# Splitting the first projection into q and k, spreading bit moves, and issuing two pairs of block loads later, in an attention kernel with a feed-forward part

## The chip, the cores and the metric

The kernel runs on one core of a Trainium2 chip. The metric is the device time of one execution in microseconds (us); lower is better. A core has five engines that run side by side: TensorE (PE, matrix products; its weight loads are listed apart as PEld), VectorE (DVE), ScalarE (ACT), GpSimd (POOL) and SyncE (SP, which here only issues transfers). The span of a profile is about 1.8 us shorter than the time of the same run, so spans are compared with spans and times with times.

## The reference

```python
# q, k, v: 4 batches x 8 heads x 768 x 64; proj: 64 x 6
q_bits = (einsum('bhsd,dk->bhsk', q, proj) > 0)      # 6 sign bits of each row
k_bits = (einsum('bhsd,dk->bhsk', k, proj) > 0)
mask   = bucket(q_bits)[..., :, None] == bucket(k_bits)[..., None, :]
scores = where(mask, q @ k.T / sqrt(64), -1e9)
x      = softmax(scores) @ v                          # 3072 tokens x 512
h      = x @ w_in                                     # 512 -> 2048
out    = (h * sigmoid(h)) @ w_out                     # 2048 -> 512
```

The mask is put into the score product as extra rows: the six bits of each row of q and k stand beside its 64 values (a contraction of 71 rows for the very first head, of 128 for most). So before a head's scores can be computed, its q and k must be transposed, projected by `proj`, compared with a threshold (which makes the bits), and the bits moved to their rows. Two heads make a pair; there are 16 pairs.

## The kernel before

The first head has code of its own, since nothing can run before its scores. One PSUM tile takes four projection products, for the two halves (e) of q and k (n), each 32 rows tall:

```python
def proj_first(h):
    bp = ps.tile([P, 512], F32, tag="m", name="bp_ps", bufs=3)
    for c in range(4):
        e, n = divmod(c, 2)
        x0 = (2 * h + n) * HS
        o = e * (NBIT + 1)
        nc.tensor.matmul(bp[32 * c : 32 * c + 32, 0:HS], pw[:, o : o + 32],
                         qk32[0][:, x0 : x0 + HS], start=True, stop=True)
    bt = btp.tile([P, S], F16, tag="bits", name="bits")
    nc.vector.tensor_scalar(out=bt[:, 0:HS], in0=bp[:, 0:HS], ...)   # one threshold
    return bt
# ... (cut)
t_first(0, 0, nc.scalar.copy)            # q of head 0: transposes on PE, copy on ACT
t_first(0, 1, nc.vector.tensor_copy)     # k of head 0: copy on DVE
warm_up(2)                               # products that compute nothing
bt = proj_first(0)
v_unit(0, (0,))                          # POOL: cast and sums of v
# ... casts on ACT, four bit moves on DVE, DVE, ACT and POOL (cut)

def second_head():
    bt = proj_first(1)
    # ... casts on POOL, four bit moves on DVE, v_unit (cut)
```

Later pairs are prepared in units planned between the attention units of earlier heads. For a group Q of four heads' worth of columns (two pairs), in `w0 = (Q - 1) * QST`:

```python
for i in range(4 if Q > 2 else 0):
    w1 = w0 + (5, 9, 11, 14)[i]
    plan(w1, lambda Q=Q, i=i: block_unit(2 * Q + i // 2, i % 2))   # DVE transpose of a block
plan(w0 + 20, lambda Q=Q: proj_unit(2 * Q, 2 * Q + 1))
for i in range(4):
    plan(w0 + 20, lambda Q=Q, i=i: bits_unit((2 * Q, 2 * Q + 1), i // 2, i % 2))
# ... (cut)
    plan(w0 + (20 if Q == 3 else 8) + i, lambda p=2 * Q + 2 + i: load_blocks(p))
```

A `bits_unit` is two DVE operations of 13 x 768 elements. In between, DVE also multiplies out the gates `g` of the feed-forward part, and each g frees a PSUM tile that PE needs for the next product `h_ps`. `x_unit(p)` writes the attention output of pair p, which SP then transposes into `xT` by a transfer.

Of the kernel before, what the change touches and what calls it, by code (L numbers as in the profile page):

```python
# [9 lines left out]
F32 = mybir.dt.float32  # L10
# [3 lines left out]
ALU = mybir.AluOpType  # L14
# [3 lines left out]
def kernel(  # L18
# [10 lines left out]
    nc = tc.nc  # L29
    B, H, S, D = q.shape  # L30
    NBIT = proj.shape[1]
    NT, DMODEL = out.shape
    DFF = moe_w_in.shape[1]
    P = 128
# [12 lines left out]
    cst = ctx.enter_context(tc.tile_pool(name="cst", bufs=1))  # L47
# [5 lines left out]
    nrm = ctx.enter_context(tc.tile_pool(name="nrm", bufs=2))  # L53
# [10 lines left out]
    v_sb = {}  # L64
# [21 lines left out]
    def load_blocks(p):  # L86
        b, h0 = p // 4, 2 * (p % 4)
        for n, src in (("q", q), ("k", k)):
            t = ld.tile([P, NG, 32], F32, tag=f"ld{n}", name=f"{n}_blk")
            for j in range(4):  # L90
                i, half = divmod(j, 2)
                nc.sync.dma_start(  # L92
                    out=t[32 * j : 32 * j + 32],
                    in_=src[b, h0 + i].rearrange("(r g) d -> r g d", r=32)
                    [:, :, 32 * half : 32 * half + 32])
            qk_sb[p, n] = t
# [18 lines left out]
    pw = cst.tile([P, 40], F32, name="pw")  # L115
# [7 lines left out]
    def warm_up(n):  # L123
        for _ in range(n):
            nc.tensor.matmul(wps, warm, warm[:, None, :].to_broadcast([P, 4, P]),  # L125
                             start=True, stop=True)
# [7 lines left out]

    NR = 2 * NBIT + 1
    BIG = 1e30
    sc = cst.tile([P, 3], F32, name="sc")
    for j, val in enumerate((0.0, 0.5, 1.0)):
        nc.vector.memset(sc[:, j : j + 1], val)
    for c in range(4):  # L140
        one = (-BIG, 0.0) if c % 2 == 0 else (BIG, 0.25 * NBIT)
        for n, val in ((NBIT + 1, one), (NBIT, (0.0, 0.5))):
            for j in range(2):
                nc.vector.memset(sc[32 * c : 32 * c + n, j : j + 1], val[j])
        if c % 2:
            nc.vector.memset(sc[32 * c : 32 * c + NBIT, 2:3], 0.0)

# [4 lines left out]
    NVS = 8  # L152
    VV = [cst.tile([P, NJ, E1], F16, name=f"vv{i}") for i in range(NVS)]
    VS = [cst.tile([P, 2, E1], F16, name=f"vs{i}") for i in range(NVS // 2)]
# [36 lines left out]
    HS = S // 2  # L191

    def t_first(h, n, copy):
        if (h, n) == (0, 0):
            qk32[0] = t32.tile([P, 2 * S], F32, tag="qk32", name="qk32")
        tp = ps.tile([P, 512], F32, tag="m", name="tp_ps", bufs=3)
        for j in range(NJ // 2):
            nc.tensor.transpose(tp[:, j * P : (j + 1) * P],  # L198
                                qk_sb[0, "qk"[n]][:, h, j * P : (j + 1) * P], ident)
        x0 = (2 * h + n) * HS  # L200
        copy(out=qk32[0][:, x0 : x0 + HS], in_=tp[:, 0:HS])

    def halves(t, r, n, e):

        return t[r, n * S : (n + 1) * S].rearrange("d (x e c) -> d x e c", e=2, c=P)[:, :, e]

    def cast_first(h, n, e, eng):
        dst = halves(QKA[0], slice(0, D), n, e) if h == 0 else \
            halves(QKB[0], slice(D, 2 * D), n, e)
        x0 = (2 * h + n) * HS  # L210
        src = qk32[0][e * D : (e + 1) * D, x0 : x0 + HS].rearrange("d (x c) -> d x c", c=P)
        if eng is nc.scalar:
            eng.mul(dst, src, CS)
        else:
            eng.tensor_scalar(out=dst, in0=src, scalar1=CS, scalar2=1.0,
                              op0=ALU.mult, op1=ALU.mult)

    def proj_first(h):

        bp = ps.tile([P, 512], F32, tag="m", name="bp_ps", bufs=3)  # L220
        for c in range(4):
            e, n = divmod(c, 2)
            x0 = (2 * h + n) * HS
            o = e * (NBIT + 1)
            nc.tensor.matmul(bp[32 * c : 32 * c + 32, 0:HS], pw[:, o : o + 32],  # L225
                             qk32[0][:, x0 : x0 + HS], start=True, stop=True)
        bt = btp.tile([P, S], F16, tag="bits", name="bits")
        nc.vector.tensor_scalar(out=bt[:, 0:HS], in0=bp[:, 0:HS],
                                scalar1=sc[:, 0:1], scalar2=sc[:, 1:2],
                                op0=ALU.is_gt, op1=ALU.subtract)  # L230
        return bt

    def bits_first(bt, h, n, e, copy):
        c = 2 * e + n
        r = slice(32 * c, 32 * c + NBIT + 1)
        dst = halves(QKA[0], slice(D, D + NBIT + 1), n, e) if h == 0 else \
            halves(QKB[0], slice(0, NBIT + 1), n, e)
        copy(out=dst, in_=bt[r, 0:HS].rearrange("d (x c) -> d x c", c=P))  # L238

    def block_unit(p, n):  # L240
        if n == 0:
            qk32[p] = t32.tile([P, 2 * S], F32, tag="qk32", name="qk32")

        dst = qk32[p][:, n * S : (n + 1) * S].rearrange(
            "p (t r a) -> p a t r", t=NJ, r=32, a=4)
        nc.vector.transpose(out=dst, in_=qk_sb[p, "qk"[n]])  # L246

    def cast_unit(p, par):
        sl = p % NSL
        dst, rows = ((QKA[sl], slice(0, 64)), (QKB[sl], slice(64, 128)))[par]  # L250
        nc.gpsimd.tensor_scalar(out=dst[rows, :], in0=qk32[p][rows, :],  # L251
                                scalar1=CS, scalar2=1.0,
                                op0=ALU.mult, op1=ALU.mult)

    def v_unit(p, heads=(0, 1)):
        for i in heads:
            h = 2 * p + i
            vv, vs = VV[h % NVS], VS[p % (NVS // 2)]
            src = v_sb[p][:, i, :].rearrange("p (t d) -> p t d", d=D)
            nc.gpsimd.tensor_copy(out=vv[:, :, 0:D], in_=src)  # L260
            sa = nrm.tile([P, 3, D], F32, tag="vsa", name="vsa")
            nc.gpsimd.tensor_tensor(out=sa, in0=src[:, 0:3], in1=src[:, 3:6], op=ALU.add)  # L262
            sb = nrm.tile([P, D], F32, tag="vsb", name="vsb")
            nc.gpsimd.tensor_tensor(out=sb, in0=sa[:, 0], in1=sa[:, 1], op=ALU.add)
            nc.gpsimd.tensor_tensor(out=vs[:, i, 0:D], in0=sb, in1=sa[:, 2], op=ALU.add)

    bits = {}

# [229 lines left out]

    t_first(0, 0, nc.scalar.copy)
    t_first(0, 1, nc.vector.tensor_copy)  # L500
    warm_up(2)
    bt = proj_first(0)
    v_unit(0, (0,))
    for e in range(2):
        for n in range(2):
            cast_first(0, n, e, nc.scalar)
    for e in range(2):
        for n in range(2):
            bits_first(bt, 0, n, e, (nc.vector.tensor_copy, nc.vector.tensor_copy,
                                     nc.scalar.copy, nc.gpsimd.tensor_copy)[2 * e + n])  # L510
    t_first(1, 0, nc.vector.tensor_copy)
    t_first(1, 1, nc.vector.tensor_copy)
    warm_up(3)

    def second_head():
        bt = proj_first(1)
        for e in range(2):
            for n in range(2):
                cast_first(1, n, e, nc.gpsimd)
                bits_first(bt, 1, n, e, nc.vector.tensor_copy)  # L520
        v_unit(0, (1,))

    at = {}
# [1 line left out]
    def plan(w, fn):  # L525
        at.setdefault(w, []).append(fn)


    plan(1, second_head)
    for i in range(3):  # L530
        plan(4 + 2 * i, lambda i=i: t_unit(1, i))
    for i in range(2):
        plan(8, lambda i=i: cast_unit(1, i))
        plan(8, lambda i=i: v_unit(1, (i,)))
# [28 lines left out]
    for Q in range(2, NQUAD):  # L563
        w0 = (Q - 1) * QST
        for i in range(4 if Q > 2 else 0):
            w1 = w0 + (5, 9, 11, 14)[i]
            plan(w1, lambda Q=Q, i=i: block_unit(2 * Q + i // 2, i % 2))
            if i % 2:
                for par in range(2):
                    plan(w1, lambda p=2 * Q + i // 2, par=par: cast_unit(p, par))  # L570
        plan(w0 + 20, lambda Q=Q: proj_unit(2 * Q, 2 * Q + 1))
        for i in range(4):
            plan(w0 + 20,
                 lambda Q=Q, i=i: bits_unit((2 * Q, 2 * Q + 1), i // 2, i % 2))
        for i in range(2):
            plan(w0 + 5 + i, lambda p=2 * Q + i: load_v(p))
            for j in range(2):
                plan(w0 + 18 + 9 * i + 2 * j, lambda p=2 * Q + i, j=j: v_unit(p, (j,)))
            if Q + 1 < NQUAD:
                plan(w0 + (20 if Q == 3 else 8) + i, lambda p=2 * Q + 2 + i: load_blocks(p))  # L580
    for p in range(NPAIR):
        plan((30, 42, 58)[p] if p < 3 else 2 * NU * (p + 1) + (2 if p % 4 == 3 else 9),
             lambda p=p: x_unit(p))
# [5 lines left out]
    for w in range(NW):  # L589
# [9 lines left out]
        n = -(-(len(moeq) - keep) // left) if len(moeq) > keep else 0  # L599
# [3 lines left out]
        if n == 1 and len(moeq) - keep < left and skip:  # L603
            n = 0
# [43 lines left out]
```

## Time and profile before

| | before |
|---|---|
| time, 3 runs | 307.0 us median (306.68 to 307.44) |
| the profiled run and its span | 308.2 us, span 306.4 us |
| PE busy | 299.8 us, 98% of the span |
| DVE, ACT, POOL busy | 59%, 69%, 42% |
| PE idle before h_ps | 1.03 us at 66.85 and 1.38 us at 76.14 |
| first scores, first exponentials, first u products | 7.94, 8.35, 9.00 us |

PE is nearly always busy, so DVE, ACT or POOL time matters only where PE stands still for it.

### The profile page before, as it was taken

The page shows a single profiled execution, that of the slowest core. Times are in us where ns is not written, and L with a number is a line of the kernel's source. Part 1 is how long each engine was busy: PE and PEld are TensorE (multiplying, and loading weights), DVE is VectorE, ACT ScalarE, POOL GpSimd, SP SyncE. Part 2 cuts the span into 40 slices and gives each one's busy share as a digit, 9 for nine tenths or more (in the row PEclk, how much of TensorE's full clock was granted, in tenths as well). Part 3 has the DMA queues.
Part 4 walks back from the last instruction along what each step waited for, and adds up shares of the span by engine and source line. Part 5 has one row for each costly group of instructions (what it writes and reads, how often), then busy time and mean ns, then how long its engine had stood idle before and what let it go on. Part 6 is the DMA issues. An engine that isn't in the chain of part 4 may idle for free.

```text
span 306.4 us, 7166 instructions
## 1 busy us (share of the span) xinstructions
PE 299.8 (98%) x2710; PEld 174.8 (57%) x2710; DVE 181.8 (59%) x342; ACT 210.2 (69%) x391; POOL 128.9 (42%) x203
## 2 busy tenths in 40 slices
PE   8999999988999999999999999999999999999996
PEld 3675855544666555545565665545566664446653
DVE  5797977789559534854597325864453342664332
ACT  5887989987777686878876666778877731543200
POOL 7589999368514842765138431675111100000000
PEclk9999999999999999999999999999999999999999
DMA  7999797999939825774048434111022013001112
GB/s 201 243 263 208 139 134 115 184 247 169 167 91 174 153 65 158 125 135 127 9 92 131 89 64 148 52 41 33 2 60 62 0 37 94 34 2 68 36 60 76
DMA packets 102786, 32.87 MB, mean 107 GB/s; under 512 B 90656, under 2 KB 99808, under 8 KB 102752
## 3 DMA queue, kind: packets, MB, share of 16 engines
q1 hardware_dynamic: 98368, 28.22, 42.8%
q0 software_dynamic: 4224, 4.19, 9.2%
q8 instruction: 21, 0.34, 0.5%
q14 instruction: 13, 0.11, 0.1%
q10 hardware_dynamic: 160, 0.00, 0.0%
HBM read 27.27 MB, written 6.29 MB: 110 GB/s over the span
## 4 chain that ended last, share of the span: by engine, by line
PE 89%; DVE 4%; DMA 4%; ACT 1%; SPq 1%; issue 0%; POOL 0%; ACTq 0%; POOLq 0%
PE o_ps L455 26%; PE h_ps L423 24%; PE s_ps L333 18%; PE o_ps L365 12%; DMA k_blk<-in_k_dram 4%; PE bp_ps L279 3%; PE tp_ps L185 2%; DVE g L429 1%; PE o_ps L441 1%; PE warm_ps L125 1%; PE tp_ps L198 1%; DVE qka L310 1%; PE bp_ps L225 1%; ACT u L336 1%; SPq L92 1%; DVE qk L246 1%
## 5 line engine op out<-in xcount | busy, mean ns | idle before, releaser
L336 ACT ACTIVATE u<-s_ps 128x512 f16<-128x512 f32 x288 | 156.3, 605 | 40.3 <-PE s_ps L333 39.8
L429 DVE SCALAR_TENSOR_TENSOR g<-th,h_ps 128x512 f16<-128x512 f32 x96 | 65.1, 684 | 75.9 <-ACT th L427 75.9
L423 PE MATMUL h_ps<-xT,win 128*128 128x512 f16 (+1 forms) x512 | 97.4, 325 | 2.4 <-DVE g L429 2.4
L365 PEld LDWEIGHTS <-u 128*128 128x128 f16 x1152 | 67.5, 98 | 42.8 <-ACT u L336 11.2
L455 PE MATMUL o_ps<-wout,g 128*128 128x512 f16 x368 | 91.6, 379 | 0.0
L427 ACT ACTIVATE th<-h_ps 128x512 f32<-128x512 f32 x96 | 57.3, 597 | 39.2 <-PE h_ps L423 36.0
L365 PE MATMUL o_ps<-vv,u 128*128 128x65 f16 x1152 | 82.8, 194 | 0.2
L423 PEld LDWEIGHTS <-win 128*128 128x128 f16 x512 | 49.9, 98 | 34.3 <-issue 3.0
L385 POOL TENSOR_TENSOR x_pr<-osum,rec 128x384 f16<-128x384 f32 x23 | 19.0, 824 | 90.5 <-DVE rec L384 90.1
L455 PEld LDWEIGHTS <-g 128*128 128x128 f16 x368 | 35.8, 98 | 34.1
L333 PE MATMUL s_ps<-qkb 128*128 128x512 f16 x192 | 52.8, 326 | 0.0
L333 PE MATMUL s_ps<-qka 71*128 71x512 f16 x192 | 52.7, 327 | 0.1
L251 POOL TENSOR_SCALAR qka<-qk 64x1536 f16<-64x1536 f32 x15 | 21.9, 1462 | 13.4 <-DVE qk L246 8.3
L460 DVE TENSOR_SCALAR osb<-o_ps 128x512 f32<-128x512 f32 x23 | 15.8, 685 | 15.5 <-PE o_ps L455 15.5
L251 POOL TENSOR_SCALAR qkb<-qk 64x1536 f16<-64x1536 f32 x15 | 22.0, 1468 | 1.2
L262 POOL TENSOR_TENSOR vsa<-v_sb 128x192 f32<-128x192 f32 x32 | 19.5, 609 | 0.0
L260 POOL CAST vv<-v_sb 128x384 f16<-128x384 f32 x32 | 16.4, 514 | 0.9 <-DMA v_sb<-in_v_dram 0.5
L246 DVE STREAM_TRANSPOSE qk<-k_blk 128x768 f32<-128x768 f32 x10 | 15.7, 1575 | 1.4 <-DMA k_blk<-in_k_dram 1.4
L333 PEld LDWEIGHTS <-qka 71*128 71x128 f16 x192 | 15.4, 97 | 0.7 <-ACT qka L238 0.5
L246 DVE STREAM_TRANSPOSE qk<-q_blk 128x768 f32<-128x768 f32 x10 | 15.7, 1574 | 0.0
L333 PEld LDWEIGHTS <-qkb 128*128 128x128 f16 x192 | 15.4, 97 | 0.0
L379 DVE TENSOR_TENSOR osum<-o_ps,vsum 128x390 f32<-128x390 f32 x23 | 13.0, 565 | 2.3
(64 smaller groups left out, 165.3 us busy)
## 6 DMA issues: line engine op xcount, KB each, us to landing
out_dram<-osb SPq DMA_DIRECT2D x23, 256.0 KB
v_sb<-in_v_dram SPq DMA_DIRECT2D x15, 384.0 KB
q_blk<-in_q_dram SPq DMA_DIRECT2D x40, 96.0 KB
k_blk<-in_k_dram SPq DMA_DIRECT2D x40, 96.0 KB
win<-in_moe_w_in_dram POOLq DMA_DIRECT2D x4, 512.0 KB, 6.9
wout<-in_moe_w_out_dram POOLq DMA_DIRECT2D x4, 512.0 KB, 7.4
q_sb<-in_q_dram SPq DMA_DIRECT2D x5, 384.0 KB
k_sb<-in_k_dram SPq DMA_DIRECT2D x5, 384.0 KB
```

Source lines behind the costliest of these rows:

```text
L246: nc.vector.transpose(out=dst, in_=qk_sb[p, "qk"[n]])
L251: nc.gpsimd.tensor_scalar(out=dst[rows, :], in0=qk32[p][rows, :], scalar1=CS, scalar2=1.0, op0=ALU.mult, op1=ALU.mult)
L260: nc.gpsimd.tensor_copy(out=vv[:, :, 0:D], in_=src)
L262: nc.gpsimd.tensor_tensor(out=sa, in0=src[:, 0:3], in1=src[:, 3:6], op=ALU.add)
L333: nc.tensor.matmul(sp[:, o0 : o0 + n], t[rows, S + jt * P : S + (jt + 1) * P], t[rows, c0 : c0 + n], start=True, stop=True)
L336: nc.scalar.activation(out=u, in_=sp, func=AF.Exp, scale=ESC)
L365: nc.tensor.matmul(o_ps[h][:, c0 // P + i, :], u[:, o0 + i * P : o0 + (i + 1) * P], vv[:, jt, :], start=(not direct(h) and w % NU == 0 and ...
L385: (nc.vector if direct(h) else nc.gpsimd).tensor_tensor(out=x_pr[p][:, :, par * D : (par + 1) * D], in0=o[:, 0:NJ, 0:D], in1=rec[:, :, Non ...
L423: nc.tensor.matmul(hp[:, j, :], w_in16[:, dt, ft * P : (ft + 1) * P], xT[4 * b + dt][:, c0 : c0 + n], start=(dt == 0), stop=(dt == NDT - 1))
L427: nc.scalar.activation(out=th, in_=hp, func=AF.Tanh, scale=0.5)
L429: after.append(lambda: nc.vector.scalar_tensor_tensor(out=g[ci][:, grp * f : (grp + 1) * f, :], in0=th, scalar=1.0, in1=hp, op0=ALU.add, o ...
L455: nc.tensor.matmul(o2[tt], g[ci][:, ft, ct * P : (ct + 1) * P], w_out16[:, ft, :], start=(ft == 0), stop=(ft == NFT - 1))
```

## The change

The intent: let q of the first head go through projection, threshold and bit moves while k is still being copied; spread the eight bit moves of a group over four units instead of one, so that gates can run between them; transpose blocks one unit later; and issue the block loads of pairs 8 and 9 behind the transfer of x of pair 4. The core of the diff:

```diff
-    sc = cst.tile([P, 3], F32, name="sc")          # constants of the thresholds
+    sc = cst.tile([P, 7], F32, name="sc")
... (20 more memsets)
-    def proj_first(h):
+    def proj_first(h, n):
         bp = ps.tile([P, 512], F32, tag="m", name="bp_ps", bufs=3)
-        for c in range(4):
-            e, n = divmod(c, 2)
+        for e in range(2):
+            o = e * (NBIT + 1)
             x0 = (2 * h + n) * HS
-            o = e * (NBIT + 1)
-            nc.tensor.matmul(bp[32 * c : 32 * c + 32, 0:HS], pw[:, o : o + 32],
+            nc.tensor.matmul(bp[32 * e : 32 * e + 32, 0:HS], pw[:, o : o + 32],
                              qk32[0][:, x0 : x0 + HS], start=True, stop=True)
... (threshold of 64 partitions in place of 128)
-    warm_up(2)
-    bt = proj_first(0)
-    v_unit(0, (0,))
+    bq = proj_first(0, 0)
+    warm_up(1)
+    bk = proj_first(0, 1)
... (casts of q on ACT, of k on POOL; moves of q on POOL and ACT, of k on DVE and ACT)
+    v_sums(0, 0)                                    # behind the bits on POOL
...
     def second_head():
-        bt = proj_first(1)
+        bt = [proj_first(1, n) for n in range(2)]
...
-            w1 = w0 + (5, 9, 11, 14)[i]
+            w1 = w0 + (5, 9, 12, 15)[i]
...
-            plan(w0 + 20,
+            plan(w0 + 20 + (i if Q < 4 else 0),
                  lambda Q=Q, i=i: bits_unit((2 * Q, 2 * Q + 1), i // 2, i % 2))
...
-                plan(w0 + (20 if Q == 3 else 8) + i, lambda p=2 * Q + 2 + i: load_blocks(p))
+                plan(w0 + (28 if Q == 3 else 8) + i, lambda p=2 * Q + 2 + i: load_blocks(p))
```

More of the change, by code (lines that the diff above doesn't have):

```diff
@@ L136 @@
     BIG = 1e30
-    sc = cst.tile([P, 3], F32, name="sc")
-    for j, val in enumerate((0.0, 0.5, 1.0)):
+    sc = cst.tile([P, 7], F32, name="sc")
+    for j, val in enumerate((0.0, 0.5, 1.0, 0.0, 0.5, 0.0, 0.5)):
         nc.vector.memset(sc[:, j : j + 1], val)
@@ L144 @@
                 nc.vector.memset(sc[32 * c : 32 * c + n, j : j + 1], val[j])
+        if c < 2:
+            for m, n, val in ((3, NBIT + 1, (-BIG, 0.0, BIG, 0.25 * NBIT)),
+                              (3, NBIT, (0.0, 0.5, 0.0, 0.5))):
+                for j in range(4):
+                    nc.vector.memset(sc[32 * c : 32 * c + n, m + j : m + j + 1], val[j])
         if c % 2:
@@ L216, in cast_first @@
                               op0=ALU.mult, op1=ALU.mult)
-    def proj_first(h):
+    def proj_first(h, n):
         bp = ps.tile([P, 512], F32, tag="m", name="bp_ps", bufs=3)
-        for c in range(4):
-            e, n = divmod(c, 2)
+        for e in range(2):
+            o = e * (NBIT + 1)
             x0 = (2 * h + n) * HS
-            o = e * (NBIT + 1)
-            nc.tensor.matmul(bp[32 * c : 32 * c + 32, 0:HS], pw[:, o : o + 32],
+            nc.tensor.matmul(bp[32 * e : 32 * e + 32, 0:HS], pw[:, o : o + 32],
                              qk32[0][:, x0 : x0 + HS], start=True, stop=True)
         bt = btp.tile([P, S], F16, tag="bits", name="bits")
-        nc.vector.tensor_scalar(out=bt[:, 0:HS], in0=bp[:, 0:HS],
-                                scalar1=sc[:, 0:1], scalar2=sc[:, 1:2],
+        nc.vector.tensor_scalar(out=bt[0:64, 0:HS], in0=bp[0:64, 0:HS],
+                                scalar1=sc[0:64, 3 + 2 * n : 4 + 2 * n],
+                                scalar2=sc[0:64, 4 + 2 * n : 5 + 2 * n],
                                 op0=ALU.is_gt, op1=ALU.subtract)
@@ L233, in bits_first @@
     def bits_first(bt, h, n, e, copy):
-        c = 2 * e + n
-        r = slice(32 * c, 32 * c + NBIT + 1)
+        r = slice(32 * e, 32 * e + NBIT + 1)
         dst = halves(QKA[0], slice(D, D + NBIT + 1), n, e) if h == 0 else \
@@ L253, in cast_unit, with v_sums @@
                                 op0=ALU.mult, op1=ALU.mult)
+    def v_sums(p, i):
+        vs = VS[p % (NVS // 2)]
+        src = v_sb[p][:, i, :].rearrange("p (t d) -> p t d", d=D)
+        sa = nrm.tile([P, 3, D], F32, tag="vsa", name="vsa")
+        nc.gpsimd.tensor_tensor(out=sa, in0=src[:, 0:3], in1=src[:, 3:6], op=ALU.add)
+        sb = nrm.tile([P, D], F32, tag="vsb", name="vsb")
+        nc.gpsimd.tensor_tensor(out=sb, in0=sa[:, 0], in1=sa[:, 1], op=ALU.add)
+        nc.gpsimd.tensor_tensor(out=vs[:, i, 0:D], in0=sb, in1=sa[:, 2], op=ALU.add)
     def v_unit(p, heads=(0, 1)):
         for i in heads:
-            h = 2 * p + i
-            vv, vs = VV[h % NVS], VS[p % (NVS // 2)]
             src = v_sb[p][:, i, :].rearrange("p (t d) -> p t d", d=D)
-            nc.gpsimd.tensor_copy(out=vv[:, :, 0:D], in_=src)
-            sa = nrm.tile([P, 3, D], F32, tag="vsa", name="vsa")
-            nc.gpsimd.tensor_tensor(out=sa, in0=src[:, 0:3], in1=src[:, 3:6], op=ALU.add)
-            sb = nrm.tile([P, D], F32, tag="vsb", name="vsb")
-            nc.gpsimd.tensor_tensor(out=sb, in0=sa[:, 0], in1=sa[:, 1], op=ALU.add)
-            nc.gpsimd.tensor_tensor(out=vs[:, i, 0:D], in0=sb, in1=sa[:, 2], op=ALU.add)
+            nc.gpsimd.tensor_copy(out=VV[(2 * p + i) % NVS][:, :, 0:D], in_=src)
+            v_sums(p, i)
     bits = {}
@@ L500 @@
     t_first(0, 1, nc.vector.tensor_copy)
-    warm_up(2)
-    bt = proj_first(0)
-    v_unit(0, (0,))
+    bq = proj_first(0, 0)
+    warm_up(1)
+    bk = proj_first(0, 1)
     for e in range(2):
-        for n in range(2):
-            cast_first(0, n, e, nc.scalar)
+        cast_first(0, 0, e, nc.scalar)
+    nc.gpsimd.tensor_copy(out=VV[0][:, :, 0:D],
+                          in_=v_sb[0][:, 0, :].rearrange("p (t d) -> p t d", d=D))
     for e in range(2):
-        for n in range(2):
-            bits_first(bt, 0, n, e, (nc.vector.tensor_copy, nc.vector.tensor_copy,
-                                     nc.scalar.copy, nc.gpsimd.tensor_copy)[2 * e + n])
+        cast_first(0, 1, e, nc.gpsimd)
+    bits_first(bq, 0, 0, 0, nc.gpsimd.tensor_copy)
+    bits_first(bq, 0, 0, 1, nc.scalar.copy)
+    bits_first(bk, 0, 1, 0, nc.vector.tensor_copy)
+    bits_first(bk, 0, 1, 1, nc.scalar.copy)
+    v_sums(0, 0)
     t_first(1, 0, nc.vector.tensor_copy)
@@ L519, in second_head @@
                 cast_first(1, n, e, nc.gpsimd)
-                bits_first(bt, 1, n, e, nc.vector.tensor_copy)
+                bits_first(bt[n], 1, n, e, nc.vector.tensor_copy)
         v_unit(0, (1,))
```

## The prediction

> **What bounds the kernel now.** I read the page's busy shares first, then the chain of waits in order of time, then the timelines of the stretches where TensorE (PE) is named as having sat idle. PE is busy 299.8 of 306.4 us, and from 76 us on the chain is PE work almost without a break, so time is won only where PE stands still. There are two such places: the start, and 64 to 77 us. First the start, in the timelines of VectorE (DVE), ScalarE (ACT) and GpSimd (POOL), and of PE:
>
> ```profile
> 4.86 0.56 DVE L201 COPY qk<-tp_ps 128x384 f32<-128x384 f32 x1 [0.84 <-PE tp_ps L198]
> 6.38 0.68 DVE L228 TENSOR_SCALAR bits<-bp_ps,sc 128x384 f16<-128x384 f32 x1 [0.96 <-PE bp_ps L225]
> 7.09 0.70 DVE L238 COPY qka<-bits 7x384 f16<-7x384 f16 x2
> ...
> 5.45 1.48 ACT L213 ACTIVATE qka<-qk 64x384 f16<-64x384 f32 x3 [0.20 <-DVE qk L201]
> ...
> 6.12 0.32 POOL L265 TENSOR_TENSOR vs<-vsb,vsa 128x64 f16<-128x64 f32 x1
> ...
> 7.94 0.81 PE L333 MATMUL s_ps<-qka 71*128 71x512 f16 x4
> ```
>
> The columns are start, duration, engine, line, operation, tiles, count, and the idle time before with its releaser. One projection tile holds q and k, so its threshold waits until 6.38 for all four products; the bit moves end at 7.79 and the first scores start at 7.94. Next the middle, in the chain of waits and in the timelines of DVE and PE:
>
> ```profile
> 52.54 12.14 DMA k_blk<-in_k_dram
> 64.69 0.02 issue
> 64.71 1.57 DVE qk L246
> ...
> 74.06 0.64 DVE qkb L310
> 74.70 0.01 issue
> 74.71 0.65 DVE qkb L307
> 75.36 0.03 issue
> 75.40 0.70 DVE g L429
> 76.10 0.04 issue
> 76.14 1.02 PE h_ps L423 x4
> ```
>
> ```profile
> 66.85 1.02 PE L423 MATMUL h_ps<-xT,win 128*128 128x512 f16 x4 [1.03 <-DVE g L429]
> 76.14 1.02 PE L423 MATMUL h_ps<-xT,win 128*128 128x512 f16 x4 [1.38 <-DVE g L429]
> ```
>
> The last quarter of k of pair 7 lands at 64.69. DVE then works without a break for 11.4 us: a transpose, gates (g), a head's sums, thresholds, and all eight bit moves of pairs 6 and 7 in one block. PE needs a PSUM tile that only a g frees, and waits 1.03 and then 1.38 us. Later the page names no PE wait of any size.
>
> **What the Trainium skill says.** "DMA: Bandwidth & Descriptors", section "Queues, rings and completion order", has each DMA engine consume one ring in order and go round robin, packet by packet, between queue rows. The trace agrees: I counted its packet records. The 128-byte packets of the block loads (SP's queue) run at about 900 per us until 54 us, then at about 180 per us beside 175 per us of 1 KB weight packets (GpSimd's queue), until 64. So the late landing comes from the weight loads of w_in 2 and 3 and w_out 0, which POOL issues at 51.8 to 54.2; the blocks of pairs 8 and 9 stand behind pair 7 in the same ring. "GPSIMD Engine Reference", section "1. Specifications", has GpSimd share its SBUF interfaces with VectorE. In this trace the last bit multiplication took 0.65 us beside POOL sums, but 0.41 us for pair 6 just before; I use the slower figure.
>
> **The change part by part.** The instruction order of the built kernel, compared with this one's, shows what really moves.
>
> 1. Constants: 20 more DVE memsets (4 full columns, 16 short ones). The 16 short ones before take 0.87 us, 0.054 each, so 20 cost at most 1.1; unwaited ones start 0.015 to 0.03 apart, so 0.6 to 0.9 is likelier. DVE has 0.84 us idle before its copy at 4.86. Cost 0, at worst 0.2.
>
> 2. First head. The q projection runs right behind the transposes of k: PE is free at 4.82 (chain), and q was copied at 4.70. Four products took 0.78 in the second head (chain), so two take 0.4: done about 5.3. DVE thresholds q after its copy of k (ends 5.42): 5.45 to 6.13, as 64 partitions of 384 should take the 0.68 that 128 do. PE does one warm-up matmul, then the k products from 5.5 to 5.93. Threshold of k: 6.05 to 6.73, since back-to-back pairs start about 0.6 apart. Moves: q on ACT at 6.15 (0.51), done 6.66; k on ACT 6.75 to 7.26 and on DVE 6.75 to 7.14. POOL: v cast to 5.09, two k casts from 5.46 (before, four took 2.16, so 0.54 each) to 6.54, one q move (0.50) to 7.05. The last move ends at 7.26 instead of 7.79; scores start near 7.35, 0.55 us earlier.
>
> 3. The price. The sums of v go behind the bits on POOL. From the start of vsa to the end of vs took 1.39 us (5.05 to 6.44), so they end at 7.05 + 1.4 = 8.45. The first instruction of the attention product (the small constant matmul that reads vs, 0.17 us on the chain) cannot start before, and the u matmuls follow at about 8.7. They started at 9.00; without this wait it would have been 8.4. So 0.3 of the 0.55 us survives. From 9.00 to 50 us PE and ACT carry the chain, so I pass on 0.3.
>
> 4. Second head: two thresholds instead of one, about 0.6 us more of DVE, partly hidden because q's products are ready 0.4 earlier. The bits are wanted at 12.95 and were done at 12.52; 0.2 us later is still in time. Cost 0.
>
> 5. Block transposes one unit later: the order on DVE, PE and POOL does not change at all by this. Effect 0.
>
> 6. Bit moves one per unit. Around pairs 4 and 5 one xT copy moves ahead of two bit moves; PE is not waiting there. Around pairs 6 and 7 exactly one g moves ahead of the last two bit operations. It ran at 75.40, and its tanh was done at 71.94, so it now runs at 74.08 to 74.76, when PE is just free (76.14 - 1.38 = 74.76). That wait goes. But the second g is still behind the two bit operations: 74.70 + 0.65 + 0.65, so 76.05 to 76.73, while PE would want it at 74.80 + 1.20 = 76.0. A new wait of about 0.7 us appears. That next product starts at 76.75 instead of 77.34: gain 0.6, at most 0.8.
>
> 7. Blocks of pairs 8 and 9 behind x of pair 4. SP issued them from 57.10 to 82.19 and x at 82.29. Now SP stands still until x of head 9 is written (POOL, 70.26 to 71.08), and the blocks go out from about 72. For pairs 10 and 11 sixteen such DMAs needed 13.5 us (90.41 to 103.76); with two weight loads still in flight I take 16, so the last lands near 88 to 90. DVE wants the four tiles at 90.70, 94.59, 96.02 and 98.64, in the order in which they land (about 80, 83, 86, 90). Slack over 7 us. As they never delayed pair 7, moving them frees nothing on the path: 0.
>
> Sum: 0.3 at the start, 0.6 to 0.8 at 76 us, no loss: about 1.0 us. 307.0 - 1.0 = 306.0.
>
> **The rivals.** A: the block move is the real gain. If pairs 8 and 9 do take bandwidth from pair 7, k of pair 7 lands up to 4 us earlier, the 1.03 us wait and the rest of the second go, and the time is about 304.3. For it: the change's own title, and the overlap of their issue (57.10 on) with the landing. Against it: no packet of pairs 8 and 9 moved before 64.7, and one ring is served in order. B: the landing is a race between POOL's weight loads and SP's blocks. Some 1,500 packets of pair 7 were left when the weights began. Weights half a microsecond later would let some 400 packets by at full rate, and k would land about 2 us earlier; weights sooner would cost little, as they end at 64 anyway. Both issue times follow from the same start, so I expect them to shift alike, but this race makes the lower side of the range longer. C: the start's 0.3 us is lost by 65 us, because DVE works on from a landing that did not shift: 306.4. D: the delayed blocks stall DVE at 90 us, a microsecond or two lost: 307 to 308. The slack of 7 us speaks against it. E: the constants or the v sums eat the start's gain: 306.4.
>
> **Range and chances.** Most cases lie between C and the full sum with 0.3 us more, 305.5 to 306.5. The three runs before spread by 0.76 us, and A and B reach down to 304.3, so I set 305.0 to 306.9. Two per cent is 6.1 us, over twice all PE waits named (1.03 + 1.38 and half a microsecond of start), so faster by that much is nearly out of the question, and slower needs a stall nothing shows.
>
> **What would show it.** The first scores start at about 7.35 and the first u matmuls at about 8.7, after a wait on vs of GpSimd; if they start at 8.4, step 3 is wrong. The wait of 1.38 us before h_ps is replaced by one of about 0.7 us a product later; the 1.03 us wait stays. K of pair 7 lands at 64.4 within 0.5; a landing at 62 or before would mean A or B. DVE never waits on q or k blocks of pairs 8 and 9. From 80 us on each product starts about 1 us earlier than before, and that offset stays to the end.

## More of the kernel before

The page's list of the chain that ended last, by engine, for this kernel:

```profile
PE 89%; DVE 4%; DMA 4%; ACT 1%; SPq 1%; issue 0%; POOL 0%; ACTq 0%; POOLq 0%
```

The 4% DMA are the one landing (k of pair 7) that the prediction quotes.

## The result, and the profile after

The changed kernel takes 307.45 us (median of 4 runs, 307.07 to 307.61); the kernel before, in the same rounds, 306.84 us (4 runs, 306.62 to 307.44). The ratio is 1.0015, with a 95% interval of 0.9997 to 1.0033. A ratio here is the mean time of one kernel's runs over that of the other's of the same rounds, so it is not quite the ratio of the medians. The class "within 2%" is right. The predicted 306.0 us is not, and 307.45 lies outside the range of 305.0 to 306.9: a gain of 1.0 us was expected and none came.

The changed kernel's start, in the timelines of PE, DVE, POOL and ACT (start, duration, engine, line, operation, tiles, count, and the idle time before with its releaser):

```profile
4.99 1.19 PE L230 MATMUL bp_ps<-qk,pw 128*32 128x384 f32 x4
6.44 0.84 PE L230 MATMUL bp_ps<-qk,pw 128*32 128x384 f32 x4
8.57 0.81 PE L341 MATMUL s_ps<-qka 71*128 71x512 f16 x4
9.64 0.30 PE L373 MATMUL o_ps<-vv,u 128*128 128x65 f16 x4
10.08 1.48 PE L230 MATMUL bp_ps<-qk,pw 128*32 128x384 f32 x8
...
6.22 0.67 DVE L233 TENSOR_SCALAR bits<-bp_ps,sc 64x384 f16<-64x384 f32 x1 [0.71 <-PE bp_ps L230]
7.32 0.67 DVE L233 TENSOR_SCALAR bits<-bp_ps,sc 64x384 f16<-64x384 f32 x1 [0.43 <-PE bp_ps L230]
...
8.66 0.32 POOL L267 TENSOR_TENSOR vs<-vsb,vsa 128x64 f16<-128x64 f32 x1
```

The first scores start at 8.57 us instead of 7.94, and not at 7.35 as predicted. The two products of q (four records: each float32 product shows as two passes) take 1.19 us, those of k 0.84; the prediction had 0.4 for either. The second head's products take 1.48 us at 10.08; all four took 0.85 us before. The threshold of k at 7.32 follows its products, and it is later than the one threshold of before at 6.38.

The middle of the changed kernel, in the timelines of DVE and PE:

```profile
73.83 0.69 DVE L437 SCALAR_TENSOR_TENSOR g<-th,h_ps 128x512 f16<-128x512 f32 x1
74.54 0.39 DVE L318 COPY qkb<-bits 13x768 f16<-13x768 f16 x1
74.94 0.42 DVE L315 TENSOR_SCALAR qkb<-bits,sc 13x768 f16<-13x768 f16 x1
75.39 1.28 DVE L437 SCALAR_TENSOR_TENSOR g<-th,h_ps 128x512 f16<-128x512 f32 x2
...
74.67 1.03 PE L431 MATMUL h_ps<-xT,win 128*128 128x512 f16 x4
76.13 1.02 PE L431 MATMUL h_ps<-xT,win 128*128 128x512 f16 x4
```

One g has moved ahead of the last two bit operations, just as predicted, and neither product shows a wait: one of 0.15 us or more would stand in brackets at the end. (The second product does have a shorter one; see bits_only.) The chain that ended last has lost its DMA part:

```profile
PE 94%; DVE 2%; ACT 1%; issue 1%; POOL 0%; ACTq 0%; POOLq 0%
```

The block loads, in the timeline of SP's issues and of DVE:

```profile
70.86 1.46 SPq L408 DMA_TRANSPOSE xT<-x_pr  x1
72.41 4.27 SPq L92 DMA_DIRECT2D q_blk<-in_q_dram  x4
...
89.49 1.56 DVE L251 STREAM_TRANSPOSE qk<-q_blk 128x768 f32<-128x768 f32 x1
```

The loads of pairs 8 and 9 do start only at 72.41, behind x of pair 4, and end their issue at 88.86; DVE takes the first block at 89.49 without a wait for it.

Against the first profile of the kernel before, the exponentials of the changed kernel run 1.27 us late from the fifth one on (12.05 against 10.78), and yet its span is 1.1 us shorter. That puzzle was the first thing to settle.

### The profile page after: what moved, and what is told of

The parts are those of the page before. It is cut to its first block, busy times and chain, and to the rows that moved or that the text cites. A ratio compares the mean times of both kernels' runs of the same rounds, so it can differ in the third digit from the quotient of the medians.

```text
span 305.3 us, 7187 instructions
## 1 busy us (share of the span) xinstructions
PE 300.9 (99%) x2709; PEld 175.1 (57%) x2709; DVE 182.4 (60%) x363; ACT 209.9 (69%) x390; POOL 130.2 (43%) x205
## 4 chain that ended last, share of the span: by engine, by line
PE 94%; DVE 2%; ACT 1%; issue 1%; POOL 0%; ACTq 0%; POOLq 0%
PE h_ps L431 26%; PE o_ps L463 26%; PE s_ps L341 19%; PE o_ps L373 12%; PE bp_ps L287 3%; PE tp_ps L191 2%; PE o_ps L449 1%; PE bp_ps L230 1%; ACT u L344 1%; PE warm_ps L125 1%; PE tp_ps L204 1%; DVE g L437 1%; DVE qka L318 1%; PE o_ps L364 0%; DVE bits L293 0%
```

## The experiments

Ten kernels were run. The before runs beside the first four gave a median of 306.96 us (11 runs); the next four are compared with the same runs and one more (306.97, 12 runs). The last two kernels ran on another chip, with 11 before runs of their own (307.17).

### before_again: the kernel before, unchanged

> The kernel before, unchanged, profiled again. Its first profile took 308.2 us, 1.2 over the median of its timed runs (306.84), and held 1.03 + 1.38 us of TensorE waits behind the late landing of k of pair 7. Theory L (that landing is a race between the weight loads and the block loads, and the first profile caught it late): a profile near the median, with a span near 305.1, k of pair 7 landed before DVE wants it (no wait on k_blk), the 1.03 us wait gone and at most about 1.4 us of waits on g left. Rival (the first profile is typical and the profiler only adds time): span 306.4 again with both waits.

Measured: 306.81 us median (306.52 to 307.36), ratio 0.9992 (0.9978 to 1.0006), span 305.1. DVE and PE, in their timelines:

```profile
63.42 1.56 DVE L246 STREAM_TRANSPOSE qk<-k_blk 128x768 f32<-128x768 f32 x1
...
73.43 0.65 DVE L307 TENSOR_SCALAR qkb<-bits,sc 13x768 f16<-13x768 f16 x1
...
74.85 1.02 PE L423 MATMUL h_ps<-xT,win 128*128 128x512 f16 x4 [1.07 <-DVE g L429]
```

The transpose of k of pair 7 waits for no transfer, the PE wait near 66 us is absent, and the later one is 1.07 us instead of 1.38. In all twelve profiles the late landing is seen once, in the profile that the prediction was made from. In the packet records of that one, well over 1,000 packets of 128 bytes were left when the 1 KB weight packets began at about 53.5 us, and they then went at about 180 per us instead of 900 and more; in those of the others whose packets were counted, the larger packets of v, which stand behind k in the same queue, begin between 53 and 58 us, so k had been read by then, before the weights began or within some 4 us of it. DVE waits for it in none of the eleven. So a good part of the idle time that the prediction worked with (the 1.03 us and 0.3 of the 1.38) is not there in a usual run. This also solves the puzzle: the exponentials of the first profile are 0.22 us ahead of this one up to 65 us and 1.28 us behind it from 78 us on, so the late landing cost that one execution 1.5 us. The first scores start at 8.15 us here, against 7.94, with the same code: the start also differs from run to run. From here on, offsets are against this profile.

### start_only: the changed kernel with the middle of before

```diff
 # against the changed kernel
-            w1 = w0 + (5, 9, 12, 15)[i]
+            w1 = w0 + (5, 9, 11, 14)[i]
-            plan(w0 + 20 + (i if Q < 4 else 0),
+            plan(w0 + 20,
-                plan(w0 + (28 if Q == 3 else 8) + i, ...load_blocks(p))
+                plan(w0 + (20 if Q == 3 else 8) + i, ...load_blocks(p))
```

> The changed kernel with the middle of the kernel before (bit moves in one block, blocks and loads at their old places); only the first-head part of the change is left. Theory P (splitting the projection costs a whole pass of TensorE twice, because four 32-column products run side by side in the time of two): scores 0.6 us later, from the fifth exponential on 1.27 us later, and the time 1.3 us above before, about 308.1. Rival W (the late start is taken back at 65 us, where TensorE waits anyway): within 0.3 us of before.

Measured: 307.92 us (307.5 to 308.42), ratio 1.0027 (1.0012 to 1.0043), span 305.7. The start is not a gain of 0.3 us, but a loss of about 0.8 (0.0027 x 307); the 1.3 us expected for this run was taken from one profile and held its slow passes. Its timelines of PE and DVE:

```profile
4.85 0.84 PE L230 MATMUL bp_ps<-qk,pw 128*32 128x384 f32 x4
5.94 0.84 PE L230 MATMUL bp_ps<-qk,pw 128*32 128x384 f32 x4
...
9.59 1.49 PE L230 MATMUL bp_ps<-qk,pw 128*32 128x384 f32 x8
```

Both pairs of products take 0.84 us here, where the changed kernel's own profile had 1.19 for the first. The code is the same up to 11 us. So 0.84 is what two products cost at full speed, and the 1.19 had slow passes in it. The PE wait of 1.06 us at 75.40 is still there, as in before_again.

### middle_only: the kernel before with the changed planning

```diff
 # against before: the three planning lines of the change, nothing of the start
+            w1 = w0 + (5, 9, 12, 15)[i]
+            plan(w0 + 20 + (i if Q < 4 else 0),
+                plan(w0 + (28 if Q == 3 else 8) + i, ...load_blocks(p))
```

> The kernel before with the middle part of the change alone (bit moves one per unit, block transposes one unit later, blocks of pairs 8 and 9 behind x of pair 4). Theory P with step 6 of the prediction: 0.6 us faster than before, about 306.2. Rival W (the change gains nothing in the middle once k of pair 7 lands in time): same as before within 0.2. Rival S (the middle is what makes the changed kernel slower): 307.4 or more.

Measured: 306.37 us (305.88 to 306.65), ratio 0.9972 (0.9957 to 0.9988), span 304.7, no listed PE wait near 75 us. The planning alone gains about 0.9 us. The ratios of start_only and middle_only, +0.27% and -0.28%, add up to nothing; the change measured +0.15% with an interval of -0.03% to +0.33%, which holds that. The gain that was expected is there, and the start pays it back.

### joint_second: the changed kernel with the second head's four products in one tile again

```diff
     def second_head():
-        bt = [proj_first(1, n) for n in range(2)]
+        bt = proj_joint(1)          # proj_first of the kernel before
...
```

> The changed kernel with q and k of the second head in one projection tile again (four column groups in one pass, one threshold), the first head still split. Theory P: the four products of the second head take 0.85 us in place of 1.48, the exponentials from the fifth on are 0.63 us earlier than in the changed kernel, the time about 306.8. Rival (the second head's delay comes from the two thresholds on DVE, or is hidden): the exponentials move by less than 0.2 us, the time stays at 307.4.

Measured: 306.56 us (305.75 to 308.09), ratio 0.9987 (0.9966 to 1.0008), span 305.0. PE's timeline:

```profile
4.96 1.49 PE L230 MATMUL bp_ps<-qk,pw 128*32 128x384 f32 x4
...
10.39 0.85 PE L246 MATMUL bp_ps<-qk,pw 128*32 128x384 f32 x8
```

The second head's products take 0.85 us, not 1.48. The first line is slower than any other: two products in 1.49 us, with slow passes throughout. So the gain at the second head (0.63 us) and a slow first head, in code that start_only ran with fast passes, stand in the same profile. The interval touches 1, so this run alone proves little.

### bits_only: the kernel before with the bit moves spread, and nothing else

```diff
-            plan(w0 + 20,
+            plan(w0 + 20 + (i if Q < 4 else 0),
                  lambda Q=Q, i=i: bits_unit((2 * Q, 2 * Q + 1), i // 2, i % 2))
```

> The kernel before with only the bit moves of pairs 4 to 7 spread, one per unit. Theory G (the whole gain of the middle is the one gate that moves ahead of the last two bit operations): about 0.8 us faster than before, like middle_only, and no wait of TensorE on g at 75 us. Rival H (part of it comes from the loads): under 0.3 us faster, or a wait on g left.

Measured: 305.97 us (305.57 to 306.57), ratio 0.9963 (0.9947 to 0.9979), span 304.3. It is faster than both kernels. Its timelines of DVE and PE:

```profile
72.92 0.69 DVE L429 SCALAR_TENSOR_TENSOR g<-th,h_ps 128x512 f16<-128x512 f32 x1
73.64 0.39 DVE L310 COPY qkb<-bits 13x768 f16<-13x768 f16 x1
74.04 0.41 DVE L307 TENSOR_SCALAR qkb<-bits,sc 13x768 f16<-13x768 f16 x1
74.48 1.28 DVE L429 SCALAR_TENSOR_TENSOR g<-th,h_ps 128x512 f16<-128x512 f32 x2
...
75.23 1.02 PE L423 MATMUL h_ps<-xT,win 128*128 128x512 f16 x4
```

The exponentials run 0.14 us behind before_again until 72 us and 0.83 us ahead from 78 us on, so this one line is worth 0.97 us: nearly all of the 1.07 us wait. The wait of 0.7 us that the prediction put in its place does come, but it is small. The chain of this run, in order of time (start, duration, what), goes through the second g:

```profile
74.04 0.41 DVE qkb L307
74.45 0.03 issue
74.48 0.70 DVE g L429
75.19 0.04 issue
75.23 1.02 PE h_ps L423 x4
```

After the moved g, the two last bit operations take 0.39 + 0.41 us instead of 0.64 + 0.65, so the second g is done at about 75.17, and the product that it frees starts at 75.23: 1.47 us after the product before it (73.76), where the same work takes 1.20 in before_again (74.85 to 76.05). So PE still stands still for about 0.26 us. The exponentials agree: they are 1.09 us ahead at 76 us and 0.83 after it.

### loads_only: the kernel before with the block loads of pairs 8 and 9 later

```diff
-                plan(w0 + (20 if Q == 3 else 8) + i, ...load_blocks(p))
+                plan(w0 + (28 if Q == 3 else 8) + i, ...load_blocks(p))
```

> The kernel before with only the blocks of pairs 8 and 9 behind x of pair 4. Theory G: the same as before within 0.2 us, the wait of about 1.1 us on g still there, no wait of DVE on a block. Rival H (the change's title): k of pair 7 lands earlier, 0.5 us or more faster. Rival D of the prediction (the later blocks stall DVE at 90 us): slower by 0.5 us or more.

Measured: 306.76 us (306.38 to 307.67), ratio 0.9995 (0.9978 to 1.0012), span 305.0; the PE wait at 74.75 is 1.05 us, and no block is waited for. The offset to before_again is about -0.1 us all the way. The loads are worth nothing here, so rival A falls: the transfer in the change's own title is not where the gain is. (In an execution with the late landing the later loads were not tried; none came again.) The third part of the planning, block transposes one unit later, was built alone and not run: the built program has the same order of instructions on every engine as the kernel before.

### second_split: the kernel before with only the second head split

```diff
     def second_head():
-        bt = proj_first(1)
+        bt = [proj_split(1, n) for n in range(2)]     # as in the change, with its constants
...
```

> The kernel before with only the second head's projection split in two tiles (and the added constants). Theory P (both tiles use column groups 0 and 1, so the two products of k queue behind those of q): the eight passes take about 1.48 us in place of 0.85, every exponential from the fifth on 0.63 us later in relation to the first, the time 0.6 us above before. Rival (hidden, as step 4 of the prediction has it): within 0.2 us of before.

Measured: 307.73 us (307.12 to 308.25), ratio 1.0022 (1.0006 to 1.0039), span 305.5. PE and DVE:

```profile
9.46 1.48 PE L252 MATMUL bp_ps<-qk,pw 128*32 128x384 f32 x8
...
10.35 1.48 DVE L255 TENSOR_SCALAR bits<-bp_ps,sc 64x384 f16<-64x384 f32 x2 [1.49 <-PE bp_ps L252]
```

The exponentials are 0.20 us ahead of before_again before these products and 0.43 us behind after them: 0.63 us lost, which is 1.48 - 0.85. The timed loss, 0.0022 x 307 = 0.7 us, agrees. It is most of the 0.8 us that start_only lost. The second threshold also takes its time, but it is PE itself that is late.

### second_groups: the changed kernel with k's products on other rows of their tile

```diff
-            nc.tensor.matmul(bp[32 * e : 32 * e + 32, 0:HS], pw[:, o : o + 32],
+            r0 = 32 * e + 64 * n
+            nc.tensor.matmul(bp[r0 : r0 + 32, 0:HS], pw[:, o : o + 32],
...   (threshold and moves on the same 64 partitions)
```

> The changed kernel with k's products in column groups 2 and 3 of their own tile (two tiles and two thresholds stay). Theory P (what costs is using the same column groups twice): the second head's eight passes shrink from 1.48 us to about 0.85, the fifth exponential comes 0.63 us earlier in relation to the first, the time about 0.6 us under the changed kernel, 306.8. Rival T (two tiles or two thresholds are what costs): no more than 0.2 us.

Measured: 306.53 us (306.29 to 307.21), ratio 0.9984 (0.9969 to 0.9998), span 304.8.

```profile
9.87 0.85 PE L231 MATMUL bp_ps<-qk,pw 128*32 128x384 f32 x8
...
10.86 1.39 DVE L235 TENSOR_SCALAR bits<-bp_ps,sc 64x384 f16<-64x384 f32 x2 [1.62 <-ACT u L346]
```

The second head is still split over two tiles and two thresholds, but q's products now write rows 0 to 63 and k's rows 64 to 127, and the eight passes are back at 0.85 us. So it is the rows written, and not the number of tiles, that decides. Two thresholds still cost something: 1.39 us in place of 0.68. The bits of the second head come later, and the offset to before_again grows from 0.2 to 0.6 us near the first scores that want them. So step 4's "0.2 us later is still in time" fails too, by 0.4 us: the moves end at 13.74 instead of 12.73 in before_again. Of the 0.63 us that the second head lost, the other rows alone win back only some 0.2.

### bits_groups: bits_only with the first head split, k on the other rows

```diff
 # against bits_only
-    warm_up(2)
-    bt = proj_first(0)
+    bq = proj_first(0, 0)            # rows 0 to 63
+    bk = proj_first(0, 1)            # rows 64 to 127, no warm-up product between
...   (casts, moves and sums of v placed as in the change; second head as before)
```

> Bit moves spread as in bits_only; the first head split into q and k as in the change, but k's two products in the other two column groups, with no warm-up product between, so that the four products can run side by side again; second head joint as before. If only the serial column groups spoiled the first head, the k threshold ends no later than the joint threshold of the kernel before at the same clock, the moves end about 0.2 us earlier, and the time is 0.1 to 0.3 us under that of bits_only (ratio 0.995 to 0.9965). If the split itself has a cost (two thresholds on DVE one after the other, v sums behind the bits), the first scores start no earlier than in bits_only at the same clock and the ratio is 0.9965 to 0.998. No PE wait near 75 us in either case.

Measured: 306.1 us (305.68 to 307.3), ratio 0.9978 (0.9961 to 0.9994), span 303.9. PE and DVE:

```profile
5.97 1.39 DVE L235 TENSOR_SCALAR bits<-bp_ps,sc 64x384 f16<-64x384 f32 x2 [0.51 <-PE bp_ps L231]
...
7.84 0.81 PE L364 MATMUL s_ps<-qka 71*128 71x512 f16 x4
```

In this profile the split pays: the first scores start at 7.84, 0.31 us earlier than in before_again and 0.45 earlier than in bits_only, though only 0.10 earlier than in the first profile of before, where all passes of the first head are fast. The u products start at 8.91 against 9.22, the same 0.31. The threshold of k now follows that of q on DVE without a gap. But PE's passes became fast at about 5.5 us here and only at about 5.8 in bits_only, and k's copy ends 0.14 us earlier here (5.46 against 5.60), so some of this may be that run's luck. The times do not settle it: 1.07 us under its own before median, where bits_only was 1.00 under. One run in six, at 307.3, raises its ratio, which falls in the range expected if the split has a cost of its own. Whether a well-placed split beats bits_only stays open.

### bits_warm1: bits_only with one warm-up product in place of two

> bits_only with one warm-up product in place of two before the first projection. If the path of the start runs through the warm-up products (they occupy PE when the copy of k is done), the first projection starts up to 0.2 us earlier and the time is 0.1 to 0.2 us under bits_only (ratio about 0.9955). If the copy of k ends last anyway, nothing changes (ratio 0.9963 within 0.0008). If fewer warm-up products keep the slow clock for longer, the passes and the first matmuls take about twice as long and the time is 0.3 us or more above bits_only (ratio 0.9975 or more).

Measured: 306.0 us (305.72 to 307.55), ratio 0.9982 (0.9962 to 1.0003), span 305.7. The six runs fall in two groups: four at 305.72 to 306.04 and two at 307.45 and 307.55. The profile happened to be of the second kind, in PE's timeline:

```profile
3.98 0.87 PE L198 MATMUL tp_ps<-ident,q_row 128*128 128x128 f32 x3 [0.66 <-DMA q_row<-in_q_dram]
...
9.73 0.81 PE L333 MATMUL s_ps<-qka 71*128 71x512 f16 x4
```

Here q itself landed late (PE waits 0.66 us for it), and the passes were slow up to the first scores, which start at 9.73 us: 1.58 us behind before_again, and still 0.63 behind from 78 us on, after the usual 0.95 us of the spread bit moves. By its ratio the third expected case (0.9975 or more) would be met, but two of six runs make it so. The expectation assumed that the slow passes of one profile would be the same in all runs of a kernel. The four fast runs are no faster than bits_only, so the warm-up product does not matter in them; whether having only one makes the slow kind more frequent, six runs cannot tell.

## Why the prediction was wrong

**Step 2 failed, at the sentence "Four products took 0.78 in the second head, so two take 0.4".** The prediction divided a time that was not a sum. The four products of before run side by side: their records in the second head start about 7 ns apart, each float32 product in two passes, 0.35 us from pass to pass, 0.85 us in all. In the change, q's products and k's products each write rows 0 to 63, and two products take the same 0.84 us that four took (start_only). The Trainium skill, "TensorE: Matmul & The Clock Gate", section "Part 3: Packing small matmuls — row/col tiling", describes this: products with small outputs at different tile positions run concurrently, with starts about 4 ns apart, and the whole takes the duration of one product plus 4 ns for each further one. The trace agrees, with about 7 ns. The prediction does not name this page. second_groups shows the cause by an edit: other rows, and the same eight passes go from 1.48 back to 0.85 us. With 0.84 us in place of 0.4, q's products and the warm-up product hold PE until k's can start at 5.94 us (start_only; they were expected at 5.5), and the threshold of k runs at 6.83, 0.45 us later than the joint one at 6.38 in the kernel before. Fewer moves behind it win back some 0.3 us, and the first scores start at 8.07 against 7.94. Both profiles have fast passes throughout these products. Of this 0.13 us, 0.10 is k, which DVE copies that much later in start_only (at 4.96 against 4.86), so the split itself costs the first head about 0.03 us; loads_only, unsplit and with its k copied at 5.00, starts its scores at 8.07 too. Nothing of the expected 0.55 us is left.

**Step 4 failed, at "Cost 0".** It looked at DVE's thresholds and not at PE, which is on the path there: the second head's products cost 0.63 us more, at 10 us, in second_split, start_only and the change alike. That the bits were wanted late (12.95 us) did not help, since PE loses its time before that. And the bits are not in time either: with the rows put right, 0.4 us is still lost to DVE (second_groups).

**Step 6 was right in its mechanism; its sizes were off.** One g moves ahead, the wait of PE goes, and a smaller one appears a product later. The term "A new wait of about 0.7 us appears" is the one that was mis-sized: it was about 0.26 (1.47 - 1.20 in bits_only; 0.10 as the profile counts it, from the modelled end of the last product). It took 0.65 us for each of the last two bit operations, which measured 0.39 and 0.41, 0.5 us less together. So the gain is 0.97 us and not 0.6: 1.07 less 0.10, both as the profile counts. The prediction chose the slower figure for the operations, because of POOL's sums. But sums run beside them in bits_only too (73.22 to 74.63 on POOL), and in the profile that it read they ran beside the multiplication of 0.41 us as well (72.40 to 73.13). Why the same operations then take 0.4 us is not settled.

**One profile was taken as typical.** The wait of 1.03 us and the 1.38 were read from a run of 308.2 us, where the three timed runs had 306.68 to 307.44. The prediction's own test says that a landing of k of pair 7 at 62 or before would mean rival A or B. In the changed kernel it had been read by about 55 us in the packet records. loads_only rules out A for executions without the late landing, and before_again shows the early landing without any change. So B, the race between weights and blocks, is the rival that describes it, but as a property of single executions, not of the change. That the weights caused the late one is read from packet records, as the prediction did with the section of "DMA: Bandwidth & Descriptors" that it names; no experiment here provoked it.

**What held, and what was not reached.** Step 1: nothing waits on the added constants. Step 3's price of 0.3 us was not paid, as the early bits that it rests on did not come: the sums of v end at 8.98 us in the change, before the first exponential ends (8.98 + 0.61 = 9.59), and the u products follow that exponential at 9.64. In bits_groups, where the bits are early, they end at 8.68 and the chain does run through them to the small constant product at 8.72, as step 3 described, but the u products at 8.91 are then only as late as the first exponential makes them (8.26 + 0.61 = 8.87). Step 5 and step 7: 0, as predicted, and rivals D and E did not come. Nor did C: what the start gains or loses against before_again stands unchanged at 66 us (0.56 us of loss in start_only, 0.31 of gain in bits_groups).

The sum from profiles, against before_again: +1.05 us by the fifth exponential (0.42 for the first head, which is slow passes of that run, since start_only with the same start is 0.08 ahead of before_again there, and 0.63 for the second head), -0.98 us at 76 us. The parts measured alone in time agree: +0.8 us of start_only, of which +0.7 are second_split, and -0.9 of middle_only. The interval of the whole, -0.1 to +1.0 us, contains their sum. The prediction's sum had +0.3 and 0.6 to 0.8 of gain.

What stays open: what decides when PE's passes become fast in an execution, and whether the changed head shifts that; the cause of the one late landing; and whether bits_groups beats bits_only.

The best kernel is the kernel before with one line changed (bits_only): 305.97 us against 306.97 in the same rounds, a ratio of 0.9963.

## What to carry to other kernels

Before dividing the time of a group of small products by their number, look at the start of each record: in this kernel, products that ran side by side cost the same for two as for four, and splitting them over tiles cost PE nothing only when they still wrote different rows. When an engine is on the chain, ask of a split what it does to that engine, and not only to the one whose wait it is meant to remove. A wait that is read from one profile is worth checking in a second one, above all when the profiled run lies outside the timed runs; and where a change has several parts, the part that holds the gain can be run without the others.

## What the Trainium skill lacked or had wrong

- "TensorE: Matmul & The Clock Gate", Part 3: its figures for packing are for K or M of 32 at N = 512, with no float32 product. Here two to four float32 products of 128 x 32 by 128 x 384 side by side took 0.84 to 0.85 us, as two passes 0.34 us apart, and two pairs on the same rows took 1.48 us.
- The same page, section "Part 1: The HAM clock gate (the "warmup" mystery)": it gives a slow and a fast state and a change that moves by ±500 ns from run to run. The trace agrees in kind: the first pair of split products took 0.84, 1.19 or 1.49 us in three profiles with the same code, and warm-up products started 0.43 us apart early and 0.22 us later. Our numbers are consistent with that gate, but the granted clock that the profile reports was 1.00 from 4.5 to 8.0 us in the profile with 1.19 too, so that figure did not show it. The page says that the number of slow products varies from run to run; it gives no time for the start of a kernel like this one: first scores at 7.94, 8.15 and 8.69 us with the same code before them, of which 0.09 us is a later start of q's transposes in the last two (3.40 against 3.31).
- "DMA: Bandwidth & Descriptors", "Queues, rings and completion order": round robin by packet is stated without a rate. In the one late profile, packets of 128 bytes went at about 180 per us beside about as many weight packets of 1 KB, against 900 and more alone.
- "GPSIMD Engine Reference", section "1. Specifications": it names the interface shared with VectorE and the kinds of VectorE instruction that contend for it, but no duration. The 13 x 768 bit copy took 0.64 us in one order and 0.39 in the other, the multiplication 0.65 and 0.41, with some of POOL's sums beside both; the first of these sums took 0.77 us beside the slow ones (before_again) and 0.58 beside the fast (bits_only). No run here shows whether it is this contention.
